# Loads and weight blocks tied to matmul groups, later step preparation, zero matmuls in the prologue: a linear attention with a feed-forward layer

## The chip, the cores and the metric

One core of a Trainium2 chip runs the kernel. The metric is the device time in microseconds of one execution. Engines are named as in the profile: PE multiplies matrices (PEld loads its weights), DVE, ACT and POOL work on vectors, SP issues DMAs.

## The reference

Attention with an exponential decay per head, over 4 sequences of 768 tokens, 8 heads of 64; its output is the input of a feed-forward layer with a sine in it (3072 tokens, 512 to 2048 to 512).

```python
for b in range(nb):                      # blocks of the sequence, state carried along
    intra = (q_b k_b^T * decay_mask) v_b
    inter = (q_b * lam_pow) kv_state
    out_b = intra + inter
    kv_state = lam_block * kv_state + (k_b * rev_pow)^T v_b
x = out as [3072, 512]
h = x @ w_in
g = h + sin(alpha * h)**2 / (alpha + 1e-9)
return g @ w_out
```

## The kernel before, in words

**Attention** goes in 24 steps of 128 tokens (6 per sequence). For step s, SP loads k, q and v (256 KB each, in rings of six buffers). `prep(s)` scales k by powers of the decay (POOL) and q (POOL, or DVE with `fast=True`) and casts v (ACT), into rings of five buffers. On PE then follow:
- T(s), `att_T`: eight transposes of q and k, copied out by DVE (`qkT`)
- S(s), `att_S`: eight score matmuls, multiplied by the mask on DVE (`S_m`)
- O(s), `att_O`: the output from the state (`Zs`, 4 matmuls) and from `S_m` with v (8), cast by ACT into `xT`; and Z, the new state (8), copied out by ACT into `Zs`

**The feed-forward layer** goes in 6 chunks of 512 tokens (4 steps each). A(c, m), `grp_A`, m = 0 to 15: four matmuls with a block of w_in into one of five PSUM banks in turn; ACT takes the sine (`t`), POOL or DVE the square (`u`), DVE forms `gT`, and only then the bank is free. B(c, s4, m4), `grp_B`: four matmuls of `gT` with w_out; after the last of a bank ACT copies to `osb` and issues the store. The weights come from HBM in eight blocks, w1.0 to w1.3 and w2.0 to w2.3, by DMAs that POOL issues; w1.j is used by groups A 4j to 4j+3, w2.j by the four groups B with m4 = j.

**Order of the work.** The kernel records operations; `schedule` is a planner with assumed durations that puts those of DVE, ACT, POOL and SP in an order (by planned start), while PE's stay as recorded. Each engine then runs its list in that order. `deps` become semaphore waits; `soft` edges only count in the plan. PE's order is: prologue (steps 0 to 3, stage by stage), A0 (16 groups A of chunk 0), B0 (16 groups B of chunk 0, with steps 4 to 7 between them), A1 (groups A of chunk 1, with steps 8 to 11), then a loop over c in which a group A of chunk c+1 and a group B of chunk c take turns, with steps 12 to 23 between them.

Before, the load of step s (4 to 11) waits for weight block s-4 (`after = [wblk[s - 4]]`), all eight blocks are issued in the prologue, and step s+2 is prepared when O(s) is recorded.

Of the kernel before, what the change touches and what calls it, by code (L numbers as in the profile page):

```python
# [206 lines left out]
def bass_lightning_attn__then__act_snake_kernel(  # L207
# [30 lines left out]
    with es:  # L238
# [112 lines left out]
        def w_block(j, soft):  # L351
            if j < 4:
# [3 lines left out]
                    slot=f"w1_{j}", nbytes=700000, soft=soft)  # L356
            else:
# [3 lines left out]
                    slot=f"w2_{j2}", nbytes=700000, soft=soft)  # L361
            wblk.append(op)

        def prep(s, fast=False):
# [5 lines left out]
            rec("DVE" if fast else "POOL", lambda e: e.tensor_tensor(q2[c][:, :, :], q32[r][:, :, :], Lq_b, ALU.mult),  # L370
                0.6 if fast else 1.05, reads=[f"q32.{r}", "Lq"], writes=[f"q2.{c}"])
            rec("ACT", lambda e: e.copy(v2[c][:, :, :], v32[r][:, :, :]), 0.62,
                reads=[f"v32.{r}"], writes=[f"v2.{c}"])
            return done
# [77 lines left out]
        def grp_A(c, m):  # L452
# [11 lines left out]
            rec("ACT", lambda e: e.activation(t16[tt][:, :], m_ps[i][:, :], ACTF.Sin, scale=alpha_sb[:, m:m + 1]),  # L464
                0.7, reads=[f"m.{i}", "alpha"], writes=[f"t.{tt}"])
# [1 line left out]
            rec("DVE" if dve else "POOL",
                lambda e: e.tensor_tensor(u16[tt][:, :], t16[tt][:, :], t16[tt][:, :], ALU.mult),  # L468
                0.35 if dve else 1.05, reads=[f"t.{tt}"], writes=[f"u.{tt}"])
            rec("DVE", lambda e: e.scalar_tensor_tensor(  # L470
                out=gT[g][:, m, :], in0=u16[tt][:, :], scalar=r_sb[:, m:m + 1], in1=m_ps[i][:, :],
                op0=ALU.mult, op1=ALU.add), 0.7, reads=[f"u.{tt}", f"m.{i}", "r"], writes=[f"g.{g}.{m}"])
# [25 lines left out]
        loaded = [8]  # L498

        def prep_next(s):  # L500
            if s < NSTEP:
                prep(s)
                if loaded[0] < NSTEP:
                    load(loaded[0])
                    loaded[0] += 1

        def slot_att(base, i, per):
# [85 lines left out]
```

## Time and profile before

| | |
|---|---|
| median of 3 runs (lowest, highest) | 243.17 us (242.1, 243.72) |
| the profiled execution: its time, its span | 243.41 us, 241.2 us |
| busy: PE, DVE, ACT, POOL | 217.7, 120.4, 121.2, 142.6 us |
| granted clock of PE, mean over the span | 0.979 |
| prologue, until the first group A | 23.77 us |
| A0, B0, A1 | 15.35, 26.05, 27.45 us |
| loop; last groups B and the end | 130.73, 17.85 us |
| step loads (SP's queue), weights (POOL's) | 18.88 MB, 4.19 MB as stored |

Times inside an execution count from the first instruction of its span. A busy PE is not PE at its best, since matmuls overlap: the length of a stage against its number of matmuls says more than its busy share.

### The profile page before, as it was taken

Reading aid. Unit: us, or ns where it says so; the run is one execution under the profiler, and the core shown is the slowest. Engines: PE = TensorE matmul, PEld = TensorE weight load, DVE = VectorE, ACT = ScalarE, POOL = GpSimd, SP = SyncE. Lnnn points to the kernel's source line nnn. Section 1 sums busy time; section 2 is a strip of 40 time slices with the busy share of each in tenths; the row PEclk is TensorE's granted clock in tenths of the full one; section 3 lists DMA queues with packets and bytes.
Section 4 is the critical chain, followed back from the end, with each engine's and each line's share of the span. In section 5 each row is a group of like instructions: output and inputs, shape, how many; then the busy total and the mean of one; then the engine's idle time right before and its main releaser. Section 6 shows DMA issues by size and latency. Waiting matters only on the chain.

```text
span 241.2 us, 3938 instructions
## 1 busy us (share of the span) xinstructions
PE 217.7 (90%) x1585; PEld 107.3 (45%) x1585; DVE 120.4 (50%) x162; ACT 121.2 (50%) x215; POOL 142.6 (59%) x149
## 2 busy tenths in 40 slices
PE   0576996899885999999999999999999999999994
PEld 0354442354441544444554554454554444444441
DVE  1663399334336687645555456364464545444300
ACT  4254585234746686546645744654654555444311
POOL 3275589466468899998658775654445544554000
PEclk9999999799996799999999999999999999999999
DMA  7999999999999999999011001101101110111122
GB/s 147 218 205 211 196 196 207 205 230 220 238 285 218 201 226 209 224 249 228 1 46 43 23 23 45 43 3 43 44 2 43 46 43 2 41 46 43 43 87 87
DMA packets 82753, 29.62 MB, mean 123 GB/s; under 512 B 75552, under 2 KB 79664, under 8 KB 82736
## 3 DMA queue, kind: packets, MB, share of 16 engines
q1 hardware_dynamic: 74880, 18.88, 43.0%
q0 software_dynamic: 4224, 4.19, 10.3%
q10 hardware_dynamic: 3632, 6.31, 7.2%
q8 instruction: 12, 0.20, 0.4%
q14 instruction: 5, 0.04, 0.1%
HBM read 27.28 MB, written 6.29 MB: 139 GB/s over the span
## 4 chain that ended last, share of the span: by engine, by line
PE 71%; DMA 10%; ACT 6%; POOL 4%; SPq 4%; issue 2%; DVE 2%; ACTq 0%; POOLq 0%
PE m_ps L479 32%; PE m_ps L460 28%; DMA v_2<-in_v_dram 5%; SPq L307 4%; DMA v_5<-in_v_dram 3%; PE A_ps L401 3%; DMA v_3<-in_v_dram 2%; PE A_ps L424 2%; PE A_ps L387 2%; ACT osb L487 2%; POOL u_2 L468 1%; PE A_ps L389 1%; PE A_ps L420 1%; DVE S_m L405 1%; ACT xT L433 1%
## 5 line engine op out<-in xcount | busy, mean ns | idle before, releaser
L460 PE MATMUL m_ps<-xT,w 128*128 128x512 bf16 x384 | 98.3, 389 | 2.1 <-ACT xT L433 1.5
L479 PE MATMUL m_ps<-w,gT 128*128 128x512 bf16 x384 | 96.5, 384 | 0.7 <-ACT osb L487 0.5
L460 PEld LDWEIGHTS m_ps<-xT,w 128*128 128x128 bf16 x384 | 37.4, 100 | 48.5 <-issue 4.2
L479 PEld LDWEIGHTS m_ps<-w,gT 128*128 128x128 bf16 x384 | 34.6, 98 | 43.6 <-ACT osb L487 6.6
L405 DVE TENSOR_TENSOR S_m<-A_ps,mask 128x1024 bf16<-128x1024 f32 x24 | 29.4, 1223 | 38.7 <-PE A_ps L401 38.7
L468 POOL TENSOR_TENSOR u_0<-t_0 128x512 bf16<-128x512 bf16 x24 | 24.9, 1039 | 28.6 <-ACT t_0 L464 28.6
L468 POOL TENSOR_TENSOR u_2<-t_2 128x512 bf16<-128x512 bf16 x24 | 24.9, 1039 | 14.3 <-ACT t_2 L464 14.2
L468 POOL TENSOR_TENSOR u_1<-t_1 128x512 bf16<-128x512 bf16 x24 | 24.9, 1040 | 7.6 <-ACT t_1 L464 7.6
L464 ACT ACTIVATE t_2<-m_ps,alpha_sb 128x512 bf16<-128x512 f32 x24 | 16.5, 687 | 23.8 <-PE m_ps L460 23.8
L470 DVE SCALAR_TENSOR_TENSOR gT<-u_2,r_sb,m_ps 128x512 bf16<-128x512 bf16 x24 | 17.9, 745 | 18.5 <-POOL u_2 L468 18.5
L470 DVE SCALAR_TENSOR_TENSOR gT<-u_0,r_sb,m_ps 128x512 bf16<-128x512 bf16 x24 | 17.8, 741 | 17.1 <-POOL u_0 L468 17.0
L464 ACT ACTIVATE t_3<-m_ps,alpha_sb 128x512 bf16<-128x512 f32 x24 | 16.5, 687 | 18.2 <-PE m_ps L460 17.8
L464 ACT ACTIVATE t_1<-m_ps,alpha_sb 128x512 bf16<-128x512 f32 x24 | 16.5, 686 | 15.8 <-PE m_ps L460 15.3
L470 DVE SCALAR_TENSOR_TENSOR gT<-u_1,r_sb,m_ps 128x512 bf16<-128x512 bf16 x24 | 17.9, 745 | 7.1 <-POOL u_1 L468 7.1
L487 ACT COPY osb<-m_ps 128x512 f32<-128x512 f32 x24 | 13.8, 586 | 14.8 <-PE m_ps L479 14.2
L468 POOL TENSOR_TENSOR u_3<-t_3 128x512 bf16<-128x512 bf16 x16 | 16.6, 1040 | 7.4 <-ACT t_3 L464 7.4
L464 ACT ACTIVATE t_0<-m_ps,alpha_sb 128x512 bf16<-128x512 f32 x24 | 16.5, 687 | 9.0 <-PE m_ps L460 8.1
L392 DVE COPY qkT<-A_ps 128x1024 bf16<-128x1024 bf16 x20 | 13.8, 690 | 13.4 <-PE A_ps L389 13.3
L470 DVE SCALAR_TENSOR_TENSOR gT<-u_3,r_sb,m_ps 128x512 bf16<-128x512 bf16 x24 | 17.8, 741 | 1.5 <-POOL u_3 L468 1.2
L447 ACT CAST Zs<-Z_ps 64x256 bf16<-64x256 f32 x40 | 14.6, 366 | 0.5
L433 ACT CAST xT<-A_ps 128x512 bf16<-128x512 f32 x20 | 11.6, 579 | 5.6 <-PE A_ps L424 5.1
L401 PE MATMUL A_ps<-qkT 64*128 64x128 bf16 x192 | 10.8, 240 | 3.9 <-ACT xT L433 2.8
(169 smaller groups left out, 171.2 us busy)
## 6 DMA issues: line engine op xcount, KB each, us to landing
out_dram<-osb ACTq DMA_DIRECT2D x24, 256.0 KB, 2.0
w<-in_moe_w_in_dram POOLq DMA_DIRECT2D x4, 512.0 KB, 7.9
w<-in_moe_w_out_dram POOLq DMA_DIRECT2D x4, 512.0 KB, 18.4
k_0<-in_k_dram SPq DMA_DIRECT2D x4, 256.0 KB, 5.0
q_0<-in_q_dram SPq DMA_DIRECT2D x4, 256.0 KB, 5.0
v_0<-in_v_dram SPq DMA_DIRECT2D x4, 256.0 KB, 5.0
k_1<-in_k_dram SPq DMA_DIRECT2D x4, 256.0 KB, 4.9
q_1<-in_q_dram SPq DMA_DIRECT2D x4, 256.0 KB, 4.8
```

The costliest lines, as they stand in the source:

```text
L307: rec_load(lambda e, a=a, d=dst[r]: e.dma_start(d[:, :, :], a), [f"{nme}32.{r}"], f"{nme}{r}", 330000, after)
L392: rec("DVE", lambda e: e.tensor_copy(qkT[j][:, :, :], dst), 0.7, reads=[key], writes=[f"qkT.{j}"])
L401: last = e.matmul(A_ps[:, 4 * h + jp, :], qkT[j][rows, 4 + jp, :], qkT[j][rows, jp, :])
L405: rec("DVE", lambda e: e.tensor_tensor(S_m[j][:, :, :], A_ps[:, :, :], mask_b, ALU.mult), 1.25, reads=["S0", "S1", "mask"], writes=[f"S_m. ...
L433: rec("ACT", lambda e: e.copy(xT[x][:, :, col:col + 128], dst), 0.62, reads=[key], writes=[f"x.{x}.{s % 4}"])
L447: rec("ACT", lambda e, rows=rows, cols=cols: e.copy(Zs[j][rows, :, cols], Z_ps[rows, :, :]), 0.4, reads=["Z"], writes=[f"Zs.{j}"])
L460: last = e.matmul(m_ps[i][:, :], w1[:, kc, 128 * m:128 * (m + 1)], xT[x][:, kc, :], start=(kc == 0), stop=(kc == NKC - 1))
L464: rec("ACT", lambda e: e.activation(t16[tt][:, :], m_ps[i][:, :], ACTF.Sin, scale=alpha_sb[:, m:m + 1]), 0.7, reads=[f"m.{i}", "alpha"], w ...
L468: lambda e: e.tensor_tensor(u16[tt][:, :], t16[tt][:, :], t16[tt][:, :], ALU.mult),
L470: rec("DVE", lambda e: e.scalar_tensor_tensor(out=gT[g][:, m, :], in0=u16[tt][:, :], scalar=r_sb[:, m:m + 1], in1=m_ps[i][:, :], op0=ALU.m ...
L479: last = e.matmul(m_ps[bank][:, :], gT[g][:, m, 128 * s4:128 * (s4 + 1)], w2[:, m, :], start=(m == 0), stop=(m == NM - 1))
L487: rec("ACT", lambda e: e.copy(osb[o][:, :], m_ps[bank][:, :]), 0.6, reads=[f"m.{bank}"], writes=[f"o.{o}"])
```

## The change

It ties loads and weight blocks to single matmul groups and moves them: w1.0 to w1.3 are issued after the preparation of step 3; w2.0 to w2.3 wait for the groups A0 7, A0 13, B0 2 and B0 6. Step 4 is loaded behind w1.2, steps 5 and 6 behind A0 10 and A0 15, steps 7 to 9 and 11 behind B0 3, 7, 11 and 15, step 13 behind group 3 of A1. Steps are prepared one ahead instead of two in B0 and A1, q on DVE for steps 4 to 8. In B0, S stands behind groups 3, 7, 10 and 13 and O behind 5, 8, 11 and 15. Matmuls of zeros are put into the prologue. In chunk 1, squares 3 and 11 go to DVE, 7 and 15 to ACT. In the loop, B stands before A. The planner now lets soft edges hold back the planned start.

```diff
+                ready_at[u] = max(ready_at[u], op.start)     # soft edges, in schedule
...
+        zeros = sb("zeros", [128, 512], BF16)
+            rec("POOL", lambda e: e.memset(zeros[:, :], 0.0), 0.5, writes=["zeros"])
...
         def load(s):
-            after = [wblk[s - 4]] if 4 <= s < 12 else []
+            after = [gate[s]] if s in gate else []
...
-            dve = c in (0, NCH - 1) and m % 4 == 3
-            rec("DVE" if dve else "POOL",
+            if (c in (0, NCH - 1) and m % 4 == 3) or (c == 1 and m % 8 == 3):
+                sq_eng, sq_dur = "DVE", 0.57
+            elif c == 1 and m % 8 == 7:
+                sq_eng, sq_dur = "ACT", 0.65
+            else:
+                sq_eng, sq_dur = "POOL", 1.05
...
+        def warm(n):
+            def pe(e):
+                for _ in range(n):
+                    last = e.matmul(m_ps[2][:, :], ident[:, :], zeros[:, :])
+                return last
+            rec("PE", pe, 0.3 * n, reads=["ident", "zeros"], writes=["m.2"])
...
+        S_B, O_B = (3, 7, 10, 13), (5, 8, 11, 15)
+        W2_A, LD_A, W2_B, LD_B, LD_A1 = (7, 13), (10, 15), (2, 6), (3, 7, 11, 15), (3,)
...
-            if s == 1:
-                w_block(0, [done])
-            elif s == 2:
-                for j in range(1, 8):
-                    w_block(j, [done])
+            if s == 2:
+                for j in range(4):
+                    w_block(j, soft=[done])
             att_S(s)
+            warm(2)
             if s < 3:
                 att_T(s + 1, bank=3 if s % 2 else 4)
-            att_O(s, bank=s % 3)
-        for s in range(4, 8):
-            load(s)
+            warm(1)
+            att_O(s, bank=s % 2)
+        warm(1)
+        gate[4] = wblk[2]
+        load(4)
+        loaded[0] = 5
         for m in range(NM):
-            grp_A(0, m)
-        prep_next(4)
-        prep_next(5)
+            op = grp_A(0, m)
+            if m in W2_A:
+                w_block(4 + W2_A.index(m), after=[op])
+            if m in LD_A:
+                gate[loaded[0]] = op
+                load_next()
+        prep_next(4, fast=True)
...
+                if i in W2_B:
+                    w_block(6 + W2_B.index(i), after=[op])
+                if i in LD_B:
+                    gate[loaded[0]] = op
+                    load_next()
+                if i in S_B:
+                    s = 4 + S_B.index(i)
+                    att_S(s)
+                    prep_next(s + 1, fast=True, soft=[last_mask[0]])
+                if i in O_B:
+                    s = 4 + O_B.index(i)
+                    att_O(s)
+                    prep_v(s + 1, soft=[P.ops[-1]])
+                    att_T(s + 1)
         for m in range(NM):                                  # A1
-            grp_A(1, m)
-            slot_att(8, m, 4)
+            op = grp_A(1, m)
+            if m in LD_A1:
+                gate[loaded[0]] = op
+                load_next()
+            if m % 4 == 0:
+                prep_next(9 + m // 4, soft=[op])
+            attend(8, m, 4, 1, 3, 0)
+            if m % 4 == 3:
+                prep_v(9 + m // 4, soft=[P.ops[-1]])
...
         for c in range(1, NCH):
             for i in range(NM):
-                if c + 1 < NCH:
-                    grp_A(c + 1, i)
-                    slot_att(4 * (c + 2), 2 * i, 8)
...
                 grp_B(c, i // 4, i % 4, bank)
                 if c + 1 < NCH:
-                    slot_att(4 * (c + 2), 2 * i + 1, 8)
+                    attend(4 * (c + 2), 2 * i, 8, 2, 6, 2)
+                    grp_A(c + 1, i)
+                    attend(4 * (c + 2), 2 * i + 1, 8, 2, 6, 2)
```

**POOL, from the prologue to the first groups of B0.** `u` are squares, `k` and `q` preparations of a step, `w` issues of weight blocks. Before, in the prologue:

```order
L368 TENSOR_TENSOR k_2<-k_2,Lk 128x512
L355 DMA w<-in_moe_w_in_dram 128x4x512
L368 TENSOR_TENSOR k_3<-k_3,Lk 128x512
L355 DMA w<-in_moe_w_in_dram 128x4x512 x3
L360 DMA w<-in_moe_w_out_dram 128x4x512 x4
L468 TENSOR_TENSOR u_0<-t_0 128x512
```

Of the change, the stretch from group 6 of A0 on (k_4 belongs to step 4, k_0<-k_5 to step 5):

```order
L486 TENSOR_TENSOR u_2<-t_2 128x512
L364 DMA w<-in_moe_w_out_dram 128x4x512
L486 TENSOR_TENSOR u_0<-t_0 128x512
L486 TENSOR_TENSOR u_1<-t_1 128x512
L486 TENSOR_TENSOR u_2<-t_2 128x512
L372 TENSOR_TENSOR k_4<-k_4,Lk 128x512
L486 TENSOR_TENSOR u_0<-t_0 128x512
L486 TENSOR_TENSOR u_1<-t_1 128x512
L364 DMA w<-in_moe_w_out_dram 128x4x512
L486 TENSOR_TENSOR u_2<-t_2 128x512
L364 DMA w<-in_moe_w_out_dram 128x4x512
L372 TENSOR_TENSOR k_0<-k_5,Lk 128x512
```

The w_out blocks now stand among the squares of A0, and the k of step 4 ahead of the squares of groups 12 to 14, where before it came behind all squares of A0.

**ACT, in A0 and B0.** `t` are sines, `v` casts. Before, the last four sines of A0 and what follows:

```order
L464 ACTIVATE t_0<-m_ps,alpha_sb 128x512
L464 ACTIVATE t_1<-m_ps,alpha_sb 128x512
L464 ACTIVATE t_2<-m_ps,alpha_sb 128x512
L464 ACTIVATE t_3<-m_ps,alpha_sb 128x512
L372 CAST v_4<-v_4 128x512
L372 CAST v_0<-v_5 128x512
```

Of the change, from the sine of group 8 on:

```order
L474 ACTIVATE t_0<-m_ps,alpha_sb 128x512
L474 ACTIVATE t_1<-m_ps,alpha_sb 128x512
L382 CAST v_4<-v_4 128x512
L474 ACTIVATE t_2<-m_ps,alpha_sb 128x512
L474 ACTIVATE t_3<-m_ps,alpha_sb 128x512
```

The cast of step 4 moved from behind sine 15 to between sines 9 and 10.

**ACT, in A1.** v_1<-v_5 belongs to step 11, v_4<-v_3 to step 9, u_3<-t_3 is a square. Before, from the first sine of A1 on:

```order
L464 ACTIVATE t_0<-m_ps,alpha_sb 128x512
L464 ACTIVATE t_1<-m_ps,alpha_sb 128x512
L372 CAST v_1<-v_5 128x512
L464 ACTIVATE t_2<-m_ps,alpha_sb 128x512
L464 ACTIVATE t_3<-m_ps,alpha_sb 128x512
L372 CAST v_2<-v_0 128x512
```

Of the change, from the sine of group 4 on:

```order
L474 ACTIVATE t_0<-m_ps,alpha_sb 128x512
L382 CAST v_4<-v_3 128x512
L474 ACTIVATE t_1<-m_ps,alpha_sb 128x512
L474 ACTIVATE t_2<-m_ps,alpha_sb 128x512
L474 ACTIVATE t_3<-m_ps,alpha_sb 128x512
L485 ACTIVATE u_3<-t_3 128x512
```

Step 9 is cast where before steps 11 and 12 had been; step 11 now follows the sine of group 12.

More of the change, by code (lines that the diff above doesn't have):

```diff
@@ L349, in alpha_ops, with w_block @@
             rec("DVE", lambda e: e.reciprocal(r_sb[:, :], aeps_sb[:, :]), 0.2, reads=["aeps"], writes=["r"])
-        def w_block(j, soft):
+        def w_block(j, soft=(), after=()):
             if j < 4:
@@ L498, in bass_lightning_attn__then__act_snake_kernel, with prep_next, load_next, attend @@
         loaded = [8]
-        def prep_next(s):
+        S_B, O_B = (3, 7, 10, 13), (5, 8, 11, 15)
+        W2_A, LD_A, W2_B, LD_B, LD_A1 = (7, 13), (10, 15), (2, 6), (3, 7, 11, 15), (3,)
+        def prep_next(s, fast=False, soft=()):
             if s < NSTEP:
[L502 to L507, printed above, removed]
+                prep(s, fast, soft)
+                if s + 4 > 11:
+                    load_next()
+        def load_next():
+            if loaded[0] < NSTEP:
+                load(loaded[0])
+                loaded[0] += 1
+        def attend(base, i, per, at_S, at_O, ahead, fast=False):
             s = base + i // per
```

57 lines of the change are left out of this document (39 added, 18 removed).

## The prediction

> **What bounds the kernel now.** I read the slices of the page first: TensorE is busy 90% of the span, with its dents in the first half. So I cut the span by windows at the stages: A0 and B0 (first and second matrix product of token chunk 0), A1 (first product of chunk 1), the loop over the other chunks, the last B. Behind the stretch stand its length, then the busy time of PE, PEld, DVE, ACT and POOL with instruction counts, the granted clock, the DMA share and GB/s.
>
> ```profile
> 23.77:39.12 15.35, 15.35 (x64) 6.65 (x65) 10.21 (x16) 10.79 (x17) 10.70 (x11) 1.00 1.22 196
> 39.12:65.17 26.05, 22.56 (x206) 11.49 (x204) 11.19 (x14) 10.18 (x21) 16.01 (x16) 0.93 1.17 222
> 65.17:92.62 27.45, 23.51 (x200) 12.12 (x200) 16.95 (x22) 18.35 (x35) 22.27 (x24) 0.88 1.19 232
> 92.62:223.35 130.73, 130.06 (x909) 62.06 (x910) 68.83 (x91) 68.09 (x118) 81.87 (x81) 1.00 0.27 65
> 223.35:241.20 17.85, 14.68 (x68) 6.46 (x66) 1.83 (x3) 3.61 (x6) 0.11 (x1) 1.00 0.19 73
> ```
>
> The loop has 0.67 us without a matmul in 130.73: nothing to win there. The last row gives the pace: 17 groups in 14.68 us, 0.864 each. The timeline of TensorE gives the price of an attention step, and three of the holes:
>
> ```profile
> 42.83 0.40 PE L387 MATMUL A_ps<-ident,q_4 128*128 128x128 bf16 x4 [2.68 <-POOL q_4 L370]
> ...
> 65.17 1.90 PE L460 MATMUL m_ps<-xT,w 128*128 128x512 bf16 x8 [0.81 <-ACT xT L433]
> ...
> 75.79 0.61 PE L401 MATMUL A_ps<-qkT 64*128 64x128 bf16 x8 [2.80 <-ACT xT L433]
> ...
> 83.55 0.40 PE L401 MATMUL A_ps<-qkT 64*128 64x128 bf16 x8
> 83.87 1.90 PE L460 MATMUL m_ps<-xT,w 128*128 128x512 bf16 x8
> 85.61 0.39 PE L420 MATMUL A_ps<-qkT,Zs 128*128 128x128 bf16 x4
> ...
> 86.85 1.89 PE L460 MATMUL m_ps<-xT,w 128*128 128x512 bf16 x8
> ```
>
> S costs 0.32 (83.55 to 83.87), O, Z and T together 1.24 (85.61 to 86.85): 1.56 a step. B0 and A1 each hold 16 groups and four steps, 13.8 + 6.2 = 20.1 us, and took 26.05 and 27.45. In B0 3.49 us are idle, in A1 3.94; the rest is the clock. Its changes lie multiples of 3.41 us apart, so I cut there:
>
> ```profile
> 40.58:43.99 3.41, 1.16 (x12) 0.75 (x12) 2.11 (x4) 0.37 (x1) 2.20 (x3) 1.00 1.11 218
> 43.99:47.40 3.41, 3.41 (x16) 1.21 (x15) 1.42 (x2) 0.60 (x2) 2.04 (x2) 0.50 0.93 208
> ...
> 64.47:67.88 3.41, 2.71 (x19) 1.23 (x20) 1.06 (x2) 3.10 (x6) 0.77 (x2) 1.00 1.05 273
> 71.29:74.70 3.41, 1.09 (x5) 0.31 (x4) 2.73 (x5) 1.62 (x4) 3.27 (x4) 1.00 1.22 217
> 74.70:81.53 6.83, 5.74 (x41) 3.08 (x42) 4.09 (x5) 5.30 (x11) 5.46 (x6) 0.50 1.27 220
> ```
>
> A stretch with PE busy 1.16 or 1.09 of 3.41 is followed by half clock; one with 2.71 is not. Half clock cost 1.7 us in B0 (half of 3.41) and 2.9 in A1 (half of 5.74). The hole of A1 goes back to a load:
>
> ```profile
> 70.97 0.62 ACT L372 CAST v_1<-v_5 128x512 bf16<-128x512 f32 x1 [3.17 <-DMA v_5<-in_v_dram]
> ```
>
> ACT stood 3.17 us on the v of step 11, with the sines of groups 2 and 3 behind it, though PE wants that v only at group 15, for O(11). DMA runs at 196 to 232 GB/s through all three stages: what matters is the order in which loads come, and who stands behind a late one.
>
> **The change, part by part.** The profiled execution took 243.41 us, 2.2 outside its span of 241.2; the median shown is 243.17. I sum against 243.41.
>
> *Prologue.* Rows of TensorE, then one of DVE and one of POOL:
>
> ```profile
> 15.32 0.59 PE L420 MATMUL m_ps<-qkT,Zs 128*128 128x128 bf16 x4 [0.57 <-ACT Zs L447]
> ...
> 16.62 0.61 PE L401 MATMUL A_ps<-qkT 64*128 64x128 bf16 x8
> ...
> 18.64 0.59 PE L420 MATMUL m_ps<-qkT,Zs 128*128 128x128 bf16 x4 [0.45 <-DVE S_m L405]
> ```
>
> ```profile
> 17.27 1.23 DVE L405 TENSOR_TENSOR S_m<-A_ps,mask 128x1024 bf16<-128x1024 f32 x1 [0.21 <-PE A_ps L401]
> ```
>
> ```profile
> 15.43 1.03 POOL L368 TENSOR_TENSOR k_3<-k_3,Lk 128x512 bf16<-128x512 f32 x1 [1.66 <-DMA k_3<-in_k_dram]
> ```
>
> The same eight matmuls take 0.61 here and 0.40 at 83.55: half clock, whatever the column says before its first change. O(1) at 15.32 hangs on loads and stays. Behind it, O, Z and S up to the mask take 1.95 us (15.32 to 17.27), half of that at full clock; over two turns that is up to 1.9. Against it: a zero matmul of 512 columns has no row in this prologue; a matmul of that size takes 0.216 at the loop's pace (0.864 / 4), twice that at half clock, and two of them stand ahead of T, one ahead of O, so at half clock A0 would start up to 0.9 later. I take A0 at 22.5 instead of 23.77; the ends are 24.7 and the landing of the first weight block. That block now leaves POOL after k_3, at 16.46. Three DMA views, and the first SP issue rows of the chain:
>
> ```profile
> w<-in_moe_w_in_dram POOLq DMA_DIRECT2D x1, 512.0 KB, 6.5
> ```
>
> ```profile
> w<-in_moe_w_out_dram POOLq DMA_DIRECT2D x1, 512.0 KB, 14.5
> ```
>
> ```profile
> w<-in_moe_w_out_dram POOLq DMA_DIRECT2D x1, 512.0 KB, 22.4
> ```
>
> ```profile
> q0 software_dynamic: 389, 0.38, 125.2%
> ```
>
> ```profile
> 18.69 2.99 POOL L360 DMA_DIRECT2D w<-in_moe_w_out_dram  x4
> ```
>
> ```profile
> v_0<-in_v_dram SPq DMA_DIRECT2D x1, 256.0 KB, 5.1
> ```
>
> ```profile
> 1.19 0.57 SPq L307
> ```
>
> The first w1 block landed 6.5 us after issue, sharing with step loads. The w2 blocks, issued 0.75 apart from 18.69, landed 14.5 (first) and 22.4 (last, issued at 20.9) later: 33.2 and 43.3, 3.4 us a block while step loads trickle beside them. Alone, 0.38 MB passed in 1.85 us, 2.6 a block. So w1.0 lands 5.7 to 6.5 after 16.46, at 22.1 to 23.0; w1.2 at 27.3. There SP is released to load step 4; the first v landed 5.1 after its issue and has two issues of about 0.5 ahead of it: v of step 4 lands at 33.5.
>
> *A0.* Full clock from the start saves 1.7; these rows of the chain show what it cost before (13 groups in 12.94), and how far a square trails its group:
>
> ```profile
> 23.77 12.94 PE m_ps L460 x52
> 36.80 0.70 ACT t_0 L464
> 37.56 0.78 POOL u_0 L468
> ```
>
> ```profile
> 36.10 1.04 POOL L468 TENSOR_TENSOR u_2<-t_2 128x512 bf16<-128x512 bf16 x1
> 37.56 1.04 POOL L468 TENSOR_TENSOR u_0<-t_0 128x512 bf16<-128x512 bf16 x1 [0.42 <-ACT t_0 L464]
> ...
> 40.55 1.22 POOL L368 TENSOR_TENSOR k_4<-k_4,Lk 128x512 bf16<-128x512 f32 x1
> ```
>
> ```profile
> 36.84 0.58 DVE L468 TENSOR_TENSOR u_3<-t_3 128x512 bf16<-128x512 bf16 x1
> 37.35 0.73 DVE L470 SCALAR_TENSOR_TENSOR gT<-u_2,r_sb,m_ps 128x512 bf16<-128x512 bf16 x1
> ```
>
> POOL has 0.42 us to spare per four groups, and gets two w2 issues (0.75 each) and k_4 (1.04) more. Worse, ACT's cast of v_4 now stands between sines 9 and 10. Sine 9 ends at 22.5 + 8.64 + 0.8 = 31.9; the cast runs 33.5 to 34.1, sine 10 to 34.8, its square to 35.9, its gT to 36.7. Group 15 takes the bank of group 10 (five banks): wanted at 35.45, it starts at 36.7. POOL goes on: k_4 to 36.9, squares 12 and 13 to 38.9, the issue of w2.1 to 39.65, square 14 to 40.65, its gT 41.4. On PE group 15 and two of B0 end at 39.55, T(4) and the third at 40.9, the fourth waits for 41.4 and ends with S(4) at 42.6. The fifth needs w2.1: 38.9 + 6.1 (between 5.7 and 6.5) = **45.0**. The 2.68 of q_4 are gone, and a wait of 2.4 for a weight block takes their place: hence what the prologue wins is swallowed.
>
> *Rest of B0.* 12 groups 10.4; S(5) to S(7) 1.0; four O/Z/T 5.0; O(5) and O(6) now stand one group (0.86) behind S, while the mask takes 1.23 and two hand-overs: 0.5 each; then the 0.81 for xT as before. 45.0 + 18.2 = 63.2, against 65.17: **-2.0**.
>
> *A1.* Steps are now prepared one ahead instead of two, so the v of step 11 stands behind sine 12 on ACT, no longer behind sine 1; loads (3 x 256 KB a step, 3.5 us at the 222 GB/s of B0) gain on a turn of 5.0, and I see no wait there. POOL was the bound in the last turns:
>
> ```profile
> 85.00:92.60 7.60, 7.09 (x76) 3.98 (x74) 6.37 (x10) 6.14 (x13) 7.60 (x9) 1.00 1.29 230
> ```
>
> Six POOL operations a turn become five, 5.0 us against PE's 3.46 + 1.56 = 5.02: no slack, so I add 0.3 a turn. 21.3 instead of 27.45: **-6.1** (ends 20.1, the floor, and 22.3, POOL's busy time in A1 before). The two ACT squares are not in the trace; I put them between the sine's 0.70 and DVE's 0.58. ACT is then busy for 18.35 + 1.3 of 21.3 us, so that cover is thin: if it goes, they cost PE up to 1.3.
>
> *Loop.* B and A change places, nothing is added. Sum: 241.2 - 2.0 - 6.1 + 2.2 = **235.3**.
>
> A rule on the clock: the Trainium skill ("TensorE: Matmul & The Clock Gate", Why this matters for your kernels) sees a drop only after idle gaps above about 3 us. Here 2.68 sufficed, so the trace disagrees; by the rule the wait of 2.4 costs no clock (235.3), by the row it can (237.0).
>
> **Rivals.**
> 1. The wait for w2.1 drops the clock as 40.58 to 43.99 did: with 0.5 + 2.4 idle it can leave 0.5 to 1.2 busy of 3.41, if the stretch falls over it. +1.7: 237.0. Against it: an idle time split over two stretches leaves each near 2.
> 2. v_4 and w2.1 come in time: A0 22.1 to 35.9, four groups, T and S to 40.2, 18.2, 21.3: A1 ends at 79.7, 230.5.
> 3. Zero matmuls don't lift the clock (S, T and O alone didn't): A0 at 24.7, 1.7 lost in it; square 13 and w2.1 follow 1.5 later: 236.8.
> 4. A POOL or ACT queue still meets a late load in A1, as at 70.97: 2.8 idle and 2.9 clock again, 241.0. For it: four output stores of 256 KB cross steps 9 and 10.
> 5. Squares and q on DVE fight POOL for a port. In rows: u_3 at 36.84 ran 0.58 beside a POOL square, k_4 at 40.55 took 0.18 longer. If each q of steps 5 to 8 instead waited out a POOL operation, 4 x 0.85 on T's path: 238.7. The Trainium skill ("SBUF — State Buffer", Who interferes with whom) has an exclusive lock there; the u_3 row speaks against it.
> 6. Slower: w2.1 lands as late as the last block did, 22.4 after issue, since two queues of step loads stand ahead: 61.3, +16.3, 251.6. It decides from 14.2 us after issue, where the 8.1 won are gone. Against it: those 22.4 were six blocks in line.
>
> **How the numbers follow.** Forecast 0.42; rivals 0.22, 0.13, 0.07, 0.08, 0.04, 0.04. 231.0 to 239.5 holds the forecast, 1, 3, 5 and the nearer half of 2: 0.8. A measurement tells 1% (2.4 us) from no change: faster 0.88 (all but 4 and 6, with a little of 4), same 0.07, slower 0.05.
>
> **What would show it.** A0 starting near 22.5 at full pace; ACT idle before the cast of v_4 at 33.5; PE idle ahead of the fifth group of B0 on w2.1; A1 in about 21 us with no idle above 1 us. Wrong it would be if w blocks or step 4 land over 2 us from the times above, or if half clock shows in A1.

## The result, and the profile after

The changed kernel takes **236.97 us**, median of 4 executions (234.56 to 238.46), against 243.0 of the kernel before on the same chip (242.1 to 243.72): ratio 0.967, 95% interval 0.961 to 0.974. Forecast were 235.3 us, in 231.0 to 239.5. The profiled execution took 234.56 us (span 232.7); two of the four show a mean granted clock of 0.993 and a span of 236.6 and lift the median, and the ratio is of the other two (234.56 and 235.55).

Stages of the changed kernel, cut as before: prologue, A0, B0, A1, loop, last B.

```profile
0.00:22.51 22.51, 12.82 (x152) 7.84 (x155) 11.47 (x18) 10.27 (x22) 9.12 (x18) 1.00 1.03 175
22.51:38.34 15.83, 14.11 (x64) 6.06 (x66) 12.40 (x17) 11.09 (x18) 12.78 (x13) 1.00 1.18 208
38.34:63.98 25.64, 21.07 (x202) 11.11 (x204) 15.45 (x18) 8.44 (x17) 10.16 (x11) 1.00 1.09 214
63.98:85.82 21.84, 20.20 (x197) 11.07 (x201) 17.40 (x24) 18.04 (x34) 18.73 (x19) 1.00 1.21 237
85.82:215.77 129.95, 129.04 (x901) 63.27 (x914) 69.73 (x91) 72.36 (x124) 83.17 (x82) 1.00 0.34 80
215.77:232.70 16.93, 13.81 (x64) 6.06 (x62) 1.92 (x3) 3.03 (x5) 0.12 (x1) 1.00 0.21 77
```

| stage | before | after | gain | forecast gain |
|---|---|---|---|---|
| prologue | 23.77 | 22.51 | 1.26 | 1.3 |
| A0 | 15.35 | 15.83 | -0.48 | with B0, 0.7 |
| B0 | 26.05 | 25.64 | 0.41 | (in the line above) |
| A1 | 27.45 | 21.84 | 5.61 | 6.1 |
| loop and last B | 148.58 | 146.88 | 1.70 | 0 |
| span | 241.20 | 232.70 | 8.50 | 8.1 |

From A0 on no stage shows half clock any more. (In the prologue the column says nothing before its first change: products still take 0.61 us at 12.64, and 0.40 only from 15.24 on.) What stays idle shows in TensorE's timeline, in A0, B0 and at A1's start (the bracket is the idle time ahead and what ended it):

```profile
35.04 1.90 PE L470 MATMUL m_ps<-xT,w 128*128 128x512 bf16 x8 [1.15 <-DVE gT L488]
37.46 1.04 PE L470 MATMUL m_ps<-xT,w 128*128 128x512 bf16 x4 [0.52 <-DVE gT L488]
...
41.70 0.81 PE L498 MATMUL m_ps<-w,gT 128*128 128x512 bf16 x3 [1.02 <-DVE gT L488]
...
45.14 1.90 PE L498 MATMUL m_ps<-w,gT 128*128 128x512 bf16 x8 [0.99 <-DMA w<-in_moe_w_out_dram]
...
63.98 1.90 PE L470 MATMUL m_ps<-xT,w 128*128 128x512 bf16 x8 [0.53 <-ACT xT L443]
```

The 2.68 us on q_4 and the 2.80 us in A1 are gone. The fifth group of B0 starts at 45.14, on w2.1, as forecast (45.0), though it idles 0.99 us and not 2.4, since the path ahead of it was late too. Two of its own holes were not forecast: 1.15 us ahead of group 13 of A0, and 1.02 ahead of the third group of B0. DVE, POOL and ACT at these places:

```profile
32.48 1.85 DVE L374 TENSOR_TENSOR q_4<-q_4,Lq 128x512 bf16<-128x512 f32 x1
34.25 0.73 DVE L488 SCALAR_TENSOR_TENSOR gT<-u_0,r_sb,m_ps 128x512 bf16<-128x512 bf16 x1
...
39.26 1.50 DVE L486 TENSOR_TENSOR u_3<-t_3 128x512 bf16<-128x512 bf16 x1 [0.54 <-ACT t_3 L474]
40.68 0.73 DVE L488 SCALAR_TENSOR_TENSOR gT<-u_1,r_sb,m_ps 128x512 bf16<-128x512 bf16 x1
...
45.34 0.68 DVE L374 TENSOR_TENSOR q_0<-q_5,Lq 128x512 bf16<-128x512 f32 x1
```

```profile
32.72 1.04 POOL L486 TENSOR_TENSOR u_1<-t_1 128x512 bf16<-128x512 bf16 x1
34.42 1.04 POOL L486 TENSOR_TENSOR u_2<-t_2 128x512 bf16<-128x512 bf16 x1 [0.66 <-ACT t_2 L474]
...
39.41 1.05 POOL L486 TENSOR_TENSOR u_2<-t_2 128x512 bf16<-128x512 bf16 x1
```

```profile
33.08 0.62 ACT L382 CAST v_4<-v_4 128x512 bf16<-128x512 f32 x1 [1.05 <-DMA v_4<-in_v_dram]
```

A square on DVE with POOL idle, late in the kernel before:

```profile
203.40 0.42 DVE L468 TENSOR_TENSOR u_3<-t_3 128x512 bf16<-128x512 bf16 x1
```

q of step 4 took 1.85 us on DVE; the q at 45.34, with POOL idle, took 0.68. The long one ended at 34.33, 0.57 after POOL's square (33.76). The square u_3 took 1.50 against 0.42 and ended 0.30 after POOL's (40.46). gT of group 8 could start only at 34.25, and group 13 takes the bank of group 8: that is the hole of 1.15. v_4's cast came at 33.08 as forecast, but it is not what group 13 waited for. The hole of 1.02 in B0 has the same cause in part: the gT at 40.68, which it waits for, stood on DVE behind that square u_3, which itself had waited 0.54 us for its sine before it met POOL.

### The profile page after: what moved, and what is told of

Read it like the earlier page. It is cut to its first block, busy times and chain, and to the rows that moved or that the text cites. A ratio compares the mean times of both kernels' runs of the same rounds, so it can differ in the third digit from the quotient of the medians.

```text
span 232.7 us, 3924 instructions
## 1 busy us (share of the span) xinstructions
PE 211.0 (91%) x1571; PEld 105.4 (45%) x1598; DVE 128.4 (55%) x169; ACT 123.2 (53%) x217; POOL 134.1 (58%) x141
## 4 chain that ended last, share of the span: by engine, by line
PE 73%; DVE 8%; DMA 5%; SPq 4%; ACT 3%; issue 2%; POOL 2%; ACTq 0%; POOLq 0%
PE m_ps L498 33%; PE m_ps L470 28%; SPq L310 4%; DVE gT L488 3%; DMA w<-in_moe_w_out_dram 3%; PE A_ps L410 3%; DVE S_m L414 3%; PE A_ps L434 2%; DMA q_3<-in_q_dram 2%; PE A_ps L396 2%; PE A_ps L398 1%; POOL u_1 L486 1%; PE A_ps L430 1%; POOL u_0 L486 1%; ACT xT L443 1%
## 5 line engine op out<-in xcount | busy, mean ns | idle before, releaser
L498 PE MATMUL m_ps<-w,gT 128*128 128x512 bf16 x377 | 94.0, 380 | 2.7 <-DVE gT L488 1.3
L470 PE MATMUL m_ps<-xT,w 128*128 128x512 bf16 x366 | 92.3, 380 | 3.8 <-DVE gT L488 1.7
L498 PEld LDWEIGHTS m_ps<-w,gT 128*128 128x128 bf16 x384 | 36.6, 98 | 46.6 <-DVE gT L488 1.7
L470 PEld LDWEIGHTS m_ps<-xT,w 128*128 128x128 bf16 x384 | 35.2, 98 | 43.0 <-DVE gT L488 3.1
L486 POOL TENSOR_TENSOR u_0<-t_0 128x512 bf16<-128x512 bf16 x24 | 25.1, 1047 | 23.1 <-ACT t_0 L474 23.1
L486 POOL TENSOR_TENSOR u_1<-t_1 128x512 bf16<-128x512 bf16 x24 | 24.9, 1038 | 5.1 <-ACT t_1 L474 5.0
L486 POOL TENSOR_TENSOR u_2<-t_2 128x512 bf16<-128x512 bf16 x24 | 24.9, 1039 | 5.1 <-ACT t_2 L474 5.0
L486 POOL TENSOR_TENSOR u_3<-t_3 128x512 bf16<-128x512 bf16 x12 | 12.5, 1039 | 23.0 <-ACT t_3 L474 23.0
L474 ACT ACTIVATE t_0<-m_ps,alpha_sb 128x512 bf16<-128x512 f32 x24 | 16.5, 687 | 15.3 <-PE m_ps L470 15.2
L410 PE MATMUL A_ps<-qkT 64*128 64x128 bf16 x192 | 10.0, 226 | 2.0 <-DVE qkT L401 1.9
```

The source lines that it names most:

```text
L410: last = e.matmul(A_ps[:, 4 * h + jp, :], qkT[j][rows, 4 + jp, :], qkT[j][rows, jp, :])
L470: last = e.matmul(m_ps[i][:, :], w1[:, kc, 128 * m:128 * (m + 1)], xT[x][:, kc, :], start=(kc == 0), stop=(kc == NKC - 1))
L486: return e.tensor_tensor(u16[tt][:, :], t16[tt][:, :], t16[tt][:, :], ALU.mult)
L498: last = e.matmul(m_ps[bank][:, :], gT[g][:, m, 128 * s4:128 * (s4 + 1)], w2[:, m, :], start=(m == 0), stop=(m == NM - 1))
```

## The experiments

All are compared with the kernel before, run beside them on the same chip (medians 243.3 to 243.6). Times are medians, in brackets the profiled execution's span.

**1. The prologue: zero matmuls or the place of w1.0?** The changed kernel without its zero matmuls:

```
             att_S(s)
-            warm(2)
...
-            warm(1)
             att_O(s, bank=s % 2)
-        warm(1)
```

> The change without its zero matmuls. Theory (the prologue's gain is swallowed by the wait for w2.1): A0 starts near 23.8 and its first groups run at half clock (1.7 us lost), but the fifth group of B0 comes only about 1.5 later, since it hangs on w2.1: about +1.5 us against the change. Rival (the prologue counts in full): 1.3 + 1.7, about +3.0 us. Second rival (zeros useless): 0.

Measured: 238.31 us, ratio 0.979 (0.973 to 0.984). TensorE:

```profile
15.13 0.61 PE L430 MATMUL m_ps<-qkT,Zs 128*128 128x128 bf16 x4 [0.41 <-ACT Zs L457]
...
23.50 12.87 PE L470 MATMUL m_ps<-xT,w 128*128 128x512 bf16 x52 [0.47 <-ACT xT L443]
39.45 4.45 PE L470 MATMUL m_ps<-xT,w 128*128 128x512 bf16 x12 [3.07 <-DVE gT L488]
```

Without them the attention products run at half clock (0.61 for a product that takes 0.40 in the changed kernel, at 15.24), A0 starts at 23.50, 0.99 us later, and its first 13 groups take 12.87 instead of 11.38. So the zeros do lift the clock. The hole before group 13 has grown to 3.07; experiment 2 says why. Of the expectations the rival (the prologue counts in full) came nearer: the fifth group of B0 starts at 48.62, 3.5 us later and not 1.5, A1 at 66.68 instead of 63.98, and the profiled span is 3.6 us longer (236.3). But 1.9 of that is the larger hole, which neither theory had.

A later run moved w1.0 back to its old place, behind k of step 2, with the zeros kept (and the places of S and O in B0 and of the gates of w2.0 and w2.1 changed):

```
-        S_B, O_B = (3, 7, 10, 13), (5, 8, 11, 15)
-        W2_A, LD_A, W2_B, LD_B, LD_A1 = (7, 13), ...
+        S_B, O_B = (3, 6, 9, 12), (5, 8, 11, 14)
+        W2_A, LD_A, W2_B, LD_B, LD_A1 = (5, 9), ...
...
+            if s == 1:
+                w_block(0, soft=[done])
             if s == 2:
-                for j in range(4):
+                for j in range(1, 4):
```

> The changed kernel with three numbers changed: the first w1 block goes out behind k of step 2 (as before the change), w2.0 and w2.1 are gated to groups 5 and 9 of A0 instead of 7 and 13, and in B0 each O stands two groups behind its S (S at 3, 6, 9, 12, O at 5, 8, 11, 14). Theory: w2.1 lands by 42, so the 0.99 us ahead of the fifth group of B0 go; the waits of O on the mask (0.44, 0.45) and of A1 on xT (0.53) go: 2 to 2.5 us less, 232 to 235 us. For the lock (an operation of DVE with two inputs from SBUF waits for POOL's running operations): q of step 4 now stands between gT of groups 8 and 9 and waits for whatever POOL runs there, 0.7 us if the issue of w2.1 leaves POOL's datapath idle at that time, up to 3.8 if squares follow each other, with a hole of up to 3 us in A0 that would eat the gain.

Measured: 238.51 us, ratio 0.981 (0.977 to 0.985), worse than the changed kernel's 0.967. ACT and TensorE in its prologue:

```profile
20.32 0.62 ACT L382 CAST v<-v 128x512 bf16<-128x512 f32 x1 [3.45 <-DMA v<-in_v_dram]
```

```profile
21.46 0.38 PE L430 MATMUL m_ps<-qkT,Zs 128*128 128x128 bf16 x4 [3.55 <-ACT Zs L457]
...
26.05 9.75 PE L470 MATMUL m_ps<-xT,w 128*128 128x512 bf16 x44
```

The early weight block shares the DMA with step 3, whose v now lands at 20.3; in the changed kernel ACT casts it at 17.35. TensorE idles 3.55 us, its clock drops in spite of the zeros, and A0 starts at 26.05. The kernel before had this wait too: ACT stood 2.14 us on v of step 3 and cast it at 19.90. So the start of A0 at 22.5 needs both edits: with the other one in place, the zeros are worth 0.99 us and the later w1.0 3.54. In the kernel before the late v cost less: both copies of the state (`Zs`) ran on ACT at 17.00, ahead of the cast, where in e9 the one that TensorE waits for stands behind it, at 20.95. The places in B0 did what was expected: 41.86 to 64.70, 22.84 us instead of 25.64. The forecast total missed the prologue.

**2. What made the hole in A0: the late v_4, or DVE waiting for POOL?** Two kernels: v_4's cast behind the sine of group 14, or q of step 4 on POOL.

```
-        prep_next(4, fast=True)
+        prep_next(4, fast=True, soft=[first])     # e2; first = group 0
+        prep_v(4, soft=[op])                      # e2; op = group 15
+        prep_next(4, fast=False)                  # e3, instead
```

> The change with the cast of v of step 4 behind sine 14 on ACT instead of between sines 9 and 10; PE and POOL in the same order. Theory port (DVE's q_4 was held up to 1.2 us by POOL's squares, and that delays gT 8 and group 13): the 1.15 us hole ahead of group 13 of A0 stays, the 0.52 hole ahead of group 15 shrinks; w2.1 leaves POOL about 0.7 earlier; -0.5 us in all. Theory load (the cast waiting for v of step 4 holds the sines): both holes go, -1.5 us.

> The change with q of step 4 scaled on POOL, behind square 14, instead of on DVE between gT 7 and gT 8. Theory port: the hole ahead of group 13 goes (under 0.2), a hole of about 0.8 ahead of group 15 stays (v of step 4), w2.1 leaves POOL at the same 38.6, so the fifth group of B0 starts at 45.1 as before and the time is the same within 0.5 us; its wait for w2.1 grows from 1.0 to about 2. Theory load: the hole ahead of group 13 stays at about 1.1.

Measured: e2 235.99 us, ratio 0.966 (0.960 to 0.973); e3 236.1, 0.967 (0.960 to 0.973). In time both equal the changed kernel; the traces tell the theories apart. e2, DVE, POOL and TensorE:

```profile
32.47 3.84 DVE L374 TENSOR_TENSOR q<-q,Lq 128x512 bf16<-128x512 f32 x1
```

```profile
31.72 3.04 POOL L486 TENSOR_TENSOR u<-t 128x512 bf16<-128x512 bf16 x3
34.72 1.03 POOL L372 TENSOR_TENSOR k<-k,Lk 128x512 bf16<-128x512 f32 x1
```

```profile
37.03 4.45 PE L470 MATMUL m_ps<-xT,w 128*128 128x512 bf16 x12 [3.06 <-DVE gT L488]
...
64.00 1.90 PE L470 MATMUL m_ps<-xT,w 128*128 128x512 bf16 x8 [0.43 <-ACT xT L443]
```

With v_4 out of the way, POOL runs three squares and k_4 without a gap to 35.75, and q of step 4 takes 3.84 us, to 36.31: again 0.56 after POOL's last. In the changed kernel ACT's late cast left POOL 0.66 us without work, and in that gap q got through. The late load I held guilty of the hole shortened it. Neither expectation for e2 came: the hole did not stay at 1.15, nor did it go, but grew to 3.06, with half clock behind it (twelve matmuls in 4.45). And yet A1 starts at 64.00, as in the changed kernel (63.98): A0 ended 3.0 us later, at 41.31, and B0 made all of it up: among others, it waited only 0.24 us for w2.1. In e1 a hole as long was not made up. So the hole in A0 is a true wait, but what it costs in the total depends on what B0 waits for. e3, with q off DVE:

```profile
22.57 13.11 PE L470 MATMUL m_ps<-xT,w 128*128 128x512 bf16 x60 [0.33 <-ACT xT L443]
36.52 1.04 PE L470 MATMUL m_ps<-xT,w 128*128 128x512 bf16 x4 [0.84 <-DVE gT L488]
...
41.58 0.40 PE L396 MATMUL A_ps<-ident,q 128*128 128x128 bf16 x4 [1.99 <-POOL q L374]
42.08 3.53 PE L498 MATMUL m_ps<-w,gT 128*128 128x512 bf16 x8
```

The hole before group 13 is gone and only group 15 waits, 0.84. But T(4) then waits 1.99 us for q on POOL, and half clock follows (eight matmuls in 3.53 instead of 1.90): what A0 wins, B0 gives back.

**3. A1: squares, v's cast, or the place of all preparation?** First the squares of chunk 1 all on POOL, as before the change:

```
-            if (c in (0, NCH - 1) and m % 4 == 3) or (c == 1 and m % 8 == 3):
+            if (c in (0, NCH - 1) and m % 4 == 3) or False:
...
-            elif c == 1 and m % 8 == 7:
+            elif False:
```

> The change with all squares of chunk 1 on POOL again. Theory (POOL bounds a turn of A1 with six operations of 1.0): A1 takes 24.0 instead of 21.84, +2.2 us. Rival (POOL has cover in A1, the gain there came from loads alone): A1 within 0.5 of 21.84, and the time the same.

Measured: 234.64 us, ratio 0.964 (0.958 to 0.971). A1 runs from 64.41 to 86.07, 21.66 us against 21.84:

```profile
64.41 1.90 PE L470 MATMUL m_ps<-xT,w 128*128 128x512 bf16 x8 [0.56 <-ACT xT L443]
...
86.07 1.03 PE L498 MATMUL m_ps<-w,gT 128*128 128x512 bf16 x4
```

The three-engine squares bring nothing here. Then the kernel before with its v cast one step later, once for all steps from 11 on and once for steps 11 to 13 alone; and with k, q and v of steps 9 and later all one step later:

```
             elif i % per == per // 4 * 3:
                 att_O(s)
+                if 10 < s + 1 < NSTEP:               # e6;  e10: 10 < s + 1 < 14
+                    prep_v(s + 1, soft=[P.ops[-1]])
...
                 att_S(s)
+                if 8 <= s:                           # e7, with v as in e6 from step 9 on
+                    prep_next(s + 1, soft=[P.ops[-1]])
```

(Not shown: `prep`, two steps ahead, leaves out what these lines now do.)

> The kernel before with one thing of the change: from step 11 on, the cast of v on ACT is put just behind the step ahead of it (one step later than before); k and q on POOL stay two steps ahead. Theory of the prediction (ACT, which stood 3.17 us on v of step 11 with sines behind it, made A1's hole): the hole of 2.80 us and the half clock behind it go, A1 takes 22 to 23 us instead of 27.45, 238 to 239 us in all. Rival (POOL stood for k and q of the same step, 2.64 us on k alone, with the squares behind them): the squares of A1's first groups start at 70.1 as before, a hole of 1.5 us or more stays, A1 takes 25 us or more, 241 to 243 us.

> The kernel before with the preparation of steps 9 and later one step ahead instead of two, k and q on POOL and v on ACT; loads, weights, squares, prologue and loop order as before. If the place of the preparation carries A1's gain: A1 takes 21.5 to 22.5 us, no idle time above 1 us in it, 237.5 to 239 us. If the loads' order and gates carry it: k, q or v of steps 9 to 11 are still waited for, A1 takes 25 us or more, 241 to 243 us.

> The kernel before with the cast of v on ACT put one step later for steps 11, 12 and 13 alone, the steps whose v is cast during A1; prologue, A0, B0 and the loop's casts stay as before. Theory (the cast of v ahead of A1's sines made A1's long turns): from the mask of S(8) to the mask of S(12), 28.32 us before and 22.88 in the changed kernel, take 22.5 to 23.5 us, the loop keeps its 8.8 us a turn, and the median is 4 to 5.5 us under the kernel before, 238 to 239.5. Rival (the gates and the order of loads carry it): the stretch stays above 26 us and the median at 242 or more.

Measured: e6 244.04 us, ratio 1.002 (0.998 to 1.005); e7 243.31, 0.9995 (0.997 to 1.002); e10 243.75, 1.002 (0.999 to 1.004). None gains anything. The masks of S(8) and S(12) on DVE bracket four turns of A1; here those of before and of e10:

```profile
67.44 1.23 DVE L405 TENSOR_TENSOR S_m<-A_ps,mask 128x1024 bf16<-128x1024 f32 x1 [2.35 <-PE A_ps L401]
...
95.76 1.23 DVE L405 TENSOR_TENSOR S_m<-A_ps,mask 128x1024 bf16<-128x1024 f32 x1 [0.35 <-PE A_ps L401]
```

```profile
71.64 1.23 DVE L410 TENSOR_TENSOR S_m<-A_ps,mask 128x1024 bf16<-128x1024 f32 x1 [6.32 <-PE A_ps L406]
...
95.49 1.23 DVE L410 TENSOR_TENSOR S_m<-A_ps,mask 128x1024 bf16<-128x1024 f32 x1 [0.44 <-PE A_ps L406]
```

The four turns shrank from 28.32 to 23.85 us (22.97 in e6, 22.88 in the changed kernel), just as the theory says, but in e10 S(12) still came at the same time, since S(8) came 4.2 later. (In e6 S(12) came at 93.04, 2.7 earlier, and the loop gave 2.2 of it back: 97.90 us from S(12) to S(23) against 95.73; so too e7, with S(12) at 94.85 and 97.44 from there.) Where the gain went in e10, in its ACT and TensorE rows:

```profile
62.94 0.62 ACT L378 CAST v<-v 128x512 bf16<-128x512 f32 x1 [2.60 <-DMA v<-in_v_dram]
...
82.38 0.62 ACT L378 CAST v<-v 128x512 bf16<-128x512 f32 x1 [2.36 <-DMA v<-in_v_dram]
```

```profile
67.88 3.39 PE L465 MATMUL m_ps<-xT,w 128*128 128x512 bf16 x8 [3.29 <-ACT xT L438]
```

ACT now stands on v of step 9, ahead of the last copies of B0 and of the xT that A1 starts with: 3.29 us idle, then half clock. In the kernel before the same cast came at 60.85 after 1.02 us. It is the same mechanism one stage earlier: on ACT, a cast waits for its load with the urgent work behind it. Why that load is later is open. The edit touches no step before 11, yet the loads ran late before that already: v of step 6 is cast at 51.53 (e6 50.92) against 50.08, and v of step 9 took 5.78 us from issue to landing instead of 5.09. That freeing some steps hands the wait to others is thus a reading of these rows, not shown by them.

e7 has no wait for a load in A1, but TensorE waits for q in each turn, here in the third:

```profile
84.38 0.40 PE L392 MATMUL A_ps<-ident,q 128*128 128x128 bf16 x4 [1.25 <-POOL q L370]
```

There k and q stand behind the turn's first two squares on POOL, so T comes late four times, by 1.18 to 1.30 us, and A1 takes 25.60. The change puts them behind the group that opens the turn, and loads, gates and casts of the steps before A1 are new too. What these runs show is that in the kernel before neither v's later place nor preparation one step ahead gives the 5.6 us. Which of the change's other edits gives them is open: k's and q's place in the turn, the casts of the stage ahead, and the order and gates of the loads are left, and no run put just one of these into the kernel before.

**4. The loop's 1.7 us.** The changed kernel with A ahead of B in the loop:

```
                 if c + 1 < NCH:
+                    grp_A(c + 1, i)
                     attend(4 * (c + 2), 2 * i, 8, 2, 6, 2)
-                    grp_A(c + 1, i)
+                if i % 4 == 0:
+                    bank = next_bank()
+                grp_B(c, i // 4, i % 4, bank)
```

> The changed kernel with the loop's old order alone: each turn puts the A group before its B group again. Theory (the loop's 1.7 us come from this order): of the bank that every fourth B group takes, the old contents must be copied out by ACT first; with A first, only one A group (0.86) lies between the last B group of a turn and the first of the next, while with B first the attention products O, Z and T (1.24) lie there as well. Then the rows of B in the loop show idle time of 0.2 to 0.4 us ended by ACT's copy to osb again, the loop and tail take 148.6 us instead of 146.9, and the median is some 1.7 us above the changed kernel's, 236 to 239. Rival (the 1.7 us come from A1, which hands the loop a smaller backlog of squares, or from the last chunk): no such idle time, loop and tail stay at 146.9.

Measured: 238.13 us, ratio 0.978 (0.972 to 0.984). My theory fell: no B group waits for osb (in the kernel before two did, 0.27 and 0.26 us). Masks of S(11) to S(14):

```profile
86.81 1.22 DVE L414 TENSOR_TENSOR S_m<-A_ps,mask 128x1024 bf16<-128x1024 f32 x1 [0.50 <-PE A_ps L410]
93.65 1.22 DVE L414 TENSOR_TENSOR S_m<-A_ps,mask 128x1024 bf16<-128x1024 f32 x1 [1.63 <-PE A_ps L410]
102.06 1.22 DVE L414 TENSOR_TENSOR S_m<-A_ps,mask 128x1024 bf16<-128x1024 f32 x1 [2.27 <-PE A_ps L410]
110.69 1.22 DVE L414 TENSOR_TENSOR S_m<-A_ps,mask 128x1024 bf16<-128x1024 f32 x1 [2.48 <-PE A_ps L410]
```

A turn of the loop takes 8.63 here (102.06 to 110.69), 8.59 in the changed kernel, 8.80 in the kernel before. At the entry, from S(11) to S(12), e5 takes 6.84 against 6.06, since its first A group waits 0.80 us for its xT while a first B group has its data; but the kernel before, with A first as well, took 6.16 there, so the 1.7 us don't come from the entry. They lie between S(12) and S(23): 95.73 us in the kernel before, 94.23 in e5, 93.88 in the changed kernel. The order gives 0.35 of that, and 1.5 stays with the old order. It must come with another edit (preparation and casts in the loop are ordered anew too); which one was not tried.

The rest of this execution's loss lies in B0, which the edit doesn't touch:

```profile
46.91 3.19 PE L498 MATMUL m_ps<-w,gT 128*128 128x512 bf16 x8 [4.07 <-DMA w<-in_moe_w_out_dram]
```

A0 was quicker in it, w2.1 was issued at 38.76 and landed 1.8 us later than in the changed kernel's profile, and the wait of 4.07 brought half clock: rival 1, in an execution of nearly the same program. In the runs with these gates w2.1 took from 5.8 us (e2) to 8.1 (e5) from issue to landing, 6.5 in the changed kernel's profile; why is open.

**5. Taking the holes out.** The changed kernel with the slots and gates of B0 as in e9, the prologue left alone, and q of step 4 on DVE behind the gT of group 9, where POOL issues w2.1; then the same with two of chunk 0's squares on ACT:

```
-        S_B, O_B = (3, 7, 10, 13), (5, 8, 11, 15)
-        W2_A, LD_A, W2_B, LD_B, LD_A1 = (7, 13), ...
+        S_B, O_B = (3, 6, 9, 12), (5, 8, 11, 14)
+        W2_A, LD_A, W2_B, LD_B, LD_A1 = (5, 9), ...
...
-        prep_next(4, fast=True)
+        prep_next(4, fast=True, soft=[ops[9]])    # ops[m]: the gT of group m of A0
+        prep_v(4, soft=[ops[10]])
...
-            elif c == 1 and m % 8 == 7:                               # e12 only
+            elif (c == 1 and m % 8 == 7) or (c == 0 and m % 8 == 1):
```

> The changed kernel with the prologue as it is, w2.0 and w2.1 gated to groups 5 and 9 of A0 instead of 7 and 13, S at 3, 6, 9, 12 and O at 5, 8, 11, 14 in B0, and q of step 4 placed on DVE behind gT of group 9, beside the issue of w2.1 on POOL, v of step 4 two sines later. Theory: A0 starts at 22.5; q of step 4 takes 0.7 to 1.3 us instead of 1.85, so no hole above 0.6 in A0; w2.1 lands by 41 and B0 has no wait for it; the waits on the mask (0.44, 0.45) and on xT (0.53) go; B0 takes 22.5 to 23.5 us instead of 25.6, 230 to 233 us in all. Rival (DMA sets the length: bytes saved at one place are waited for at another): w2.3 or the loads of steps 7 and 8 come late by as much, B0 keeps 25 us, 234 to 237.

> The run of the slots and the earlier w2 with one thing more: two of chunk 0's squares (groups 1 and 9) on ACT instead of POOL. If POOL's lock on DVE still costs A0 time, two operations of 1.04 us less on POOL shorten the waits of DVE's squares and of q of step 4: A0 is 0.3 to 1 us shorter than in that run. If ACT is the tighter engine (16 sines of 0.69 and two squares of 0.63 in 14 us), the sines trail and A0 is as long or up to 0.6 longer.

Measured: e11 235.26 us, ratio 0.967 (0.964 to 0.970); e12 235.45, 0.966 (0.963 to 0.969). e11's A0 and B0:

```profile
22.50:41.57 19.07, 15.69 (x65) 6.59 (x65) 14.68 (x17) 10.98 (x18) 13.39 (x14) 0.91 1.18 206
41.57:63.58 22.01, 21.19 (x206) 11.17 (x205) 13.86 (x17) 8.20 (x17) 8.67 (x10) 1.00 1.01 202
```

```profile
30.65 3.40 DVE L486 TENSOR_TENSOR u<-t 128x512 bf16<-128x512 bf16 x1
```

```profile
30.72 3.04 POOL L486 TENSOR_TENSOR u<-t 128x512 bf16<-128x512 bf16 x3
```

B0 fell to 22.01 us, but A0 rose to 19.07: now DVE's own square, 0.57 in the kernel before, stood 3.40 us behind three squares of POOL, and TensorE idled 3.38 and dropped its clock. What was expected of B0 came, what was expected of A0 (no hole above 0.6) did not. In e12 the same square took 2.56, and its A0 18.40, as the lock has it with less on POOL; the time is the same. So in the last run nothing of two SBUF inputs is left on DVE in A0:

```
-            if (c in (0, NCH - 1) and m % 4 == 3) or (c == 1 and m % 8 == 3):
+            if (c == NCH - 1 and m % 4 == 3) or (c == 1 and m % 8 == 3):
...
-            elif c == 1 and m % 8 == 7:
+            elif (c == 1 and m % 8 == 7) or (c == 0 and m % 4 == 3):
...
-        prep_next(4, fast=True)
+        prep_next(4, soft=[ops[11]])
+        prep_v(4, soft=[ops[13]])
...
-                if i == 1:
+                if i == 2:
                     att_T(4)
```

with S at (4, 7, 10, 13), O at (6, 9, 12, 14) and w2.0, w2.1 at (5, 9).

> The run of the slots and the earlier w2, with every operation of two SBUF inputs taken off DVE in A0: chunk 0's four squares of DVE go to ACT, q of step 4 to POOL behind square 14, its v behind the last sine; T(4) stands one group later, S at 4, 7, 10, 13, O at 6, 9, 12, 14. Theory (DVE's waits in A0 are POOL's lock): no row of DVE in A0 is longer than 0.8 us, A0 takes 14 to 14.8 us from 22.5 instead of 15.8 (changed kernel) or 19.1 (the run before); B0 as there, 22 to 23 us, A1 from 59 to 60.5; 229 to 232 us in all. Rival (loads set the length): w2.2, w2.3 or the loads of steps 6 to 8 land as late as in the run before, 52.3, 57.7, 54 to 61, and what A0 gains is waited for in B0: A1 starts at 62.5 or later and the time is 233 or more.

Measured: **233.3 us** (231.72 to 234.22), ratio 0.957 (0.953 to 0.961), the fastest kernel of this study. A0, B0, A1, and one row of DVE and TensorE each:

```profile
22.42:37.63 15.21, 14.37 (x63) 5.95 (x65) 8.54 (x12) 12.22 (x20) 12.54 (x13) 1.00 1.20 207
37.63:61.68 24.05, 21.11 (x201) 10.88 (x204) 13.81 (x17) 10.01 (x20) 8.88 (x10) 1.00 1.09 215
61.68:84.64 22.96, 20.46 (x198) 11.09 (x200) 17.38 (x24) 17.61 (x33) 20.85 (x21) 1.00 1.23 236
```

```profile
55.16 0.69 DVE L374 TENSOR_TENSOR q<-q,Lq 128x512 bf16<-128x512 f32 x1 [1.67 <-DMA q<-in_q_dram]
```

```profile
55.99 0.38 PE L396 MATMUL A_ps<-ident,q 128*128 128x128 bf16 x4 [1.48 <-DVE q L374]
```

A0 takes 15.2 us (14 to 14.8 were expected), B0 24.05 (22 to 23). Both theories have a part: the lock's holes are gone, and in B0 a load is waited for. A1 starts at 61.68, 2.3 us earlier than in the changed kernel, but needs 22.96 us, 1.1 more: TensorE waits 1.25 and 0.99 us there for DVE's copy `qkT` (at 69.96 and 81.45), where the changed kernel has 0.28 and 0.84. k of step 9 reaches POOL at 62.38 instead of 61.11, so that loads set this pace too is likely, but not shown.

## Why the prediction was right, and where its steps were not

- **Start of A0, 22.5: right by value (22.51), with half of its cause.** I put all of it down to the clock. The zeros are worth 0.99 (e1). The later w1.0, which I used only to bound the landing of that block, brings v of step 3 from 19.90 to 17.35; without it the zeros don't hold the clock (e9). That the sum came out at 22.5 all the same is luck.
- **A0: the mechanism failed, the sum held.** v_4 came at 33.08 as forecast (33.5), but group 13 waited, not group 15 first, and for DVE's q behind POOL's squares. This was rival 5 with chance 0.04, and I argued it away: the square u_3 in the row at 36.84 "ran 0.58 beside a POOL square". It ended at 37.42, 0.28 after that POOL square ended at 37.14: it had waited too, by 0.16, as the same operation took 0.42 at 203.40 with POOL idle, in the profile that I had. The Trainium skill ("SBUF — State Buffer", Who interferes with whom) lets a DVE instruction with two SBUF inputs contend with a GpSimd one that reads SBUF; the rows shown here agree: products took 0.68 free and up to 3.84 beside POOL, squares 0.42 and up to 3.40. In e2 a larger hole left A1's start where it was: so a wrong path could leave the sum standing.
- **w2.1 and the fifth group of B0: right**, 45.09 and 45.14 against 45.0. The wait was 0.99, since the groups ahead ran late for the reason just named. Rival 1, half clock from that wait, did not come in the profiled execution, and did in e5's; no other execution of the changed kernel has rows to say.
- **Rest of B0: 18.84 us from 45.14 against 18.2.** The two waits of O on the mask and the one of xT were there (0.44, 0.45, 0.53). Of the 0.6 over, 0.3 is idle time (2.12 us listed against 1.81 forecast: one q held by POOL, 1.35 us at 51.53, let TensorE wait 0.54 that the sum didn't have), 0.3 the groups and steps themselves.
- **A1: 21.84 against 21.3, and its reasoning was half wrong.** "POOL has no slack" fell with e4: with six operations a turn A1 takes 21.66. The load behind ACT was real, but moving that cast alone gains nothing (e6, e10). So the forecast named the place of the wait, and the change did end it, but by which of its edits is open: the size was right without its reason being shown.
- **Loop: 0 forecast, 1.70 gained.** The term that was missed. The row I judged by (0.67 us idle in 130.73) hid 0.2 us a turn in its first turns; the period from mask to mask shows it, 8.80 against 8.59.
- **The total: partly luck.** The span came out at 232.7 against 233.1 forecast because errors cancel: A0 with B0 0.8 us late and A1 0.5 too long, against the 1.7 of the loop that nobody forecast.

## What to carry to other kernels

Read a long duration as a wait until the same operation has been seen short: the end of the other engine's operation, not the start of this one, gives the lock away. Taking a wait out of one place may show it at another; compare absolute times of the same event, not the length of the stretch that was mended. And a transfer that is issued earlier than it is needed can be paid by the one that is needed now, as v of step 3 paid for w1.0 here.

## What the runs showed of the hardware

- An elementwise operation of DVE with two SBUF inputs waits while POOL computes: the square of 0.42 and the product of 0.68 took 1.50 and 1.85 beside POOL's squares. It can lose to a whole run of POOL's operations that follow at once: 3.40 and 3.84 us behind three and four of them. It ends 0.28 to 0.30 us (bf16 square) or 0.55 to 0.57 (f32 to bf16 product) after the last one it waited for. In other places it got in between two of them, and POOL's next one took 1.22 instead of 1.04 (k_4 at 40.55 before, u_0 at 36.42 after); what decides is open. DVE's gT, with one SBUF and one PSUM input, kept its 0.73 to 0.75 beside POOL.
- TensorE's clock dropped after idle times of 1.99 us (e3) and 2.10 (e12). After 2.75 us ahead of T(4) it dropped in e7 and e10 (the next four matmuls took 1.70 and 1.81) and held in e6 (1.03). The rule that the prediction cited, a drop only above about 3 us (the Trainium skill, "TensorE: Matmul & The Clock Gate", Why this matters for your kernels), is not borne out by these rows; the idle time alone doesn't decide.
